# First two blocks of a fused attention and feed-forward kernel in halves of eight slots

## The chip, the cores and the metric

The kernel runs on one core of a Trainium2 chip. The metric is the device time of one execution in microseconds, the median of several runs. The engines are TensorE (PE, matmuls into PSUM), VectorE (DVE), ScalarE (ACT, functions by tables), GpSimd (POOL) and SyncE (SP, which issues the transfers).

## The reference

A linear attention with a complex decay, then two feed-forward layers on 3072 tokens of 384 features:

```python
scale = np.minimum(mag, 0.999) / (mag + 1e-06)      # mag = |a_re + i a_im|
for t in range(S):                                   # S = 768, B = 4, H = 8, D = 48
    S_re = ar * S_re - ai * S_im + k_t (x) v_t
    S_im = ar * S_im + ai * S_re_old
    y[:, :, t] = q_t . S_re
x = y as (3072, 384)
h = x @ w_in;  x = (h * cos(h)) @ w_out              # d_ff = 2048
h = x @ w2_in; y = (h * sigmoid(h)) @ w2_out
```

The weights come as 64-bit floats.

## The kernel before

**Attention in chunks.** Tokens go in 24 chunks of 128 (NC); chunk c belongs to batch c % 4. For a chunk, PE sums logarithms and angles over time with a triangular matrix (XL, XU: tiles pl, pu), DVE and ACT make the exponentials and the sine and cosine of the angles (FR, XE, XM, XS), DVE forms kt and qt (KQ), PE transposes them (TR: pt) and makes scores (SC: ps), DVE masks these into A, PE forms the output (YY: py) and the new state (PS: pS), and XF splits py into two 16-bit parts, xhi on ACT and xlo on DVE. ACT's exponentials and its sines use different tables, and LOGS and TRIG load them.

**Feed-forward in blocks and slots.** Three chunks make a block u of 384 tokens (8 blocks). Layer 1 of a block takes 16 slots, one for each piece f of 128 of the 2048 hidden features. In a slot, G1 makes h (nine matmuls: three pieces of the 384 features, each as hi x hi, lo x hi, hi x lo), GA takes the cosine on ACT, as a sine with a shift, GB multiplies (DVE) and rounds to ghi (ACT), GC forms the remainder glo (DVE), and two slots later G2 adds ghi and glo times w_out into three accumulators acc in PSUM (nine matmuls). h has two buffers, so h of slot s + 2 waits for glo of slot s. After f = 15, G2 copies the accumulators to o and stores them to x1d in DRAM; layer 2 reads them from there.

**Weights of layer 1.** RAW1 loads the 64-bit weights of a piece f (786 KB); DVE decodes them in three steps (lines 421, 423, 425) into wd, ACT rounds to 16 bits (line 456), DVE makes the remainder (line 466). A call `run` advances this stream by so many steps; four steps are one piece.

**Order.** PE and ACT run in the order in which the code issues. DVE, POOL and SP are ordered by a scheduler at build time, from slot 0 on. A table `plan` says what is called in which slot, half 0 ahead of G2 and half 1 behind it: chunk c starts at slot base(c), with XLU (XL, XU, FR) there, the tables, XE, XM and the next chunk's logarithms XA in half 1, the sines and KQ one slot on. TR(c - 1) and TR(c) stand relative to base: the transposes of k of chunk c at base(c + 1) - 2, those of q at base(c + 1) - 1. Before, base is 2, 6, 10, 14, 19 for chunks 4 to 8 (line 608). Tiles of the tag "a" in PSUM (pt, ps, py, pS, pl, pu, pn) share three buffers.

Of the kernel before, what the change touches and what calls it, by code (L numbers as in the profile page):

```python
# [9 lines left out]
F32 = mybir.dt.float32  # L10
# [44 lines left out]
GBUFS, WBUFS = 3, 3  # L55
SPARE = {(2, 1): 4, (2, 0): 5, (1, 2): 6, (2, 2): 7, (1, 3): 8, (1, 1): 9, (1, 6): 9, (1, 5): 10, (2, 5): 11, (2, 6): 12, (2, 3): 13, (2, 4): 14, (3, 0): 15}
LEADS = (2, 3, 4, 6, 7)
NA = 12
# [8 lines left out]
def fast_path(tc, q, k, v, a_re, a_im, w1_in, w1_out, w2_in, w2_out, out, bad_cnt):  # L67
    nc = tc.nc
    act, V, PE, G, SP = nc.scalar.activation, nc.vector, nc.tensor, nc.gpsimd, nc.sync
    with ExitStack() as ctx:  # L70
# [25 lines left out]
        x1d = dr.tile([NBLK, 128, KT, TB], F32, name="x1d")  # L96

# [149 lines left out]
        def XSP(c):  # L247
            d = st[c]
            if c < NFP:
                return  # L250
            ahi, thi = (xp.tile([128, DM], F32R, name=n, bufs=1) for n in ("ahi", "thi"))
            alo, tlo = (yp.tile([128, DM], F32R, name=n, tag=t) for n, t in (("alo", "ip"), ("tlo", "f")))
            act(out=ahi, in_=d["a1"], func=AF.Copy)
            act(out=thi, in_=d["an"], func=AF.Copy, scale=1.0 / TWO_PI)
            G.tensor_tensor(out=alo, in0=d["a1"], in1=ahi.bitcast(F32), op=ALU.subtract)
            V.scalar_tensor_tensor(out=tlo, in0=d["an"], scalar=1.0 / TWO_PI, in1=thi.bitcast(F32), op0=ALU.mult, op1=ALU.subtract)
            d["split"] = (ahi, alo, thi, tlo)
# [11 lines left out]
        def FR(c):  # L269
            d = st[c]  # L270
            pu = d["pu"]
            f = d["f"] = new(c, "f", yp)
            cs = d["cs"] = new(c, "cs", yp, cols=2 * DM).rearrange("p (h c d) -> p h c d", h=H, c=2)
            if CPU <= c < NFP:
                act(out=f, in_=pu, func=AF.Copy, bias=MAGIC)
            else:
                V.tensor_scalar(out=f, in0=pu, scalar1=MAGIC, scalar2=None, op0=ALU.add)
            V.scalar_tensor_tensor(out=f, in0=f, scalar=MAGIC, in1=pu, op0=ALU.subtract, op1=ALU.subtract)  # L278
            if c + B < NC:
                SP.dma_start(out=card[c % B:c % B + 1, :], in_=f[127:128, :])  # L280
            V.tensor_scalar(out=cs[:, :, 0].bitcast(I32), in0=hd(f).bitcast(I32), scalar1=0x7FFFFFFF, scalar2=None, op0=ALU.bitwise_and)
# [87 lines left out]
        def XF(c):  # L369
            u, cu = divmod(c, CPU)  # L370
            if cu == 0:
                xts[u] = tuple(xt.tile([128, KT, TB], F16, name=n) for n in ("xhi", "xlo"))
# [167 lines left out]
        def G2(layer, u, f, g):  # L540
            w = W[layer, f]
            if f == 0:
                acc[layer, u] = [px.tile([128, TB], F32, name=f"acc{m}") for m in range(KT)]
            for m, n in [(m, n) for m in range(KT) for n in range(2)] + [(m, 2) for m in range(KT)]:
# [5 lines left out]
                PE.matmul(out=acc[layer, u][m], lhsT=lhsT, rhs=rhs, start=(f == 0 and n == 0), stop=(f == NF - 1 and n == 2))  # L550
            if f == NF - 1:
                for m, ps in enumerate(acc.pop((layer, u))):
                    o = stage.tile([128, TB], F32, name="o", bufs=3)
                    sc = p2(SX1 - SG - SWT) if layer == 0 else p2(-SG2 - SWT)
                    if m == 1:
# [3 lines left out]
                    if layer == 0:  # L559
# [7 lines left out]
        def X1(u):  # L567
            hi, lo = (xt.tile([128, KT, TB], F16, name=n) for n in ("xhi", "xlo"))
# [39 lines left out]
        def base(c):  # L608
            return (16 * (c - CPU)) // 3 - LEADS[min(c - CPU, len(LEADS) - 1)]

# [24 lines left out]
        at(0, 1, XS, CPU)  # L635
        at(1, 0, KQ, CPU)
        for c in range(CPU, NC):
            b0 = base(c)
            if c > CPU:
                if c + 1 < NC:  # L640
                    at(b0 - 1, 1, XQ, c + 1)
                    at(b0 - 1, 1, XR, c + 1)
# [13 lines left out]
                at(b0 + YO, YH, YYS, c - 1)  # L656
                at(b0 + XFO, 1, XF, c - 1)
# [18 lines left out]
        for n in range(24):  # L676
            at(n, 0, run, 2)
            at(n, 1, run, 2)
# [23 lines left out]
        def slot(s):  # L702
            if 0 <= s < last:
                layer, r = divmod(s, 16 * NBLK)
                u, f = divmod(r, 16)
# [323 lines left out]
```

## Time and profile before

| | us |
|---|---|
| runs shown, median (lowest to highest) | 1006.39 (1005.92 to 1006.64) |
| the profiled execution | 1005.74 |
| its span, first to last instruction | 1004.0 |
| PE busy | 954.7 (95%) |
| VectorE busy | 624.2 (62%) |
| ScalarE busy | 606.9 (60%) |
| POOL busy | 114.9 (11%) |
| mean granted clock of PE | 0.986 |

The profile is taken by the hardware from one execution. The page cuts the span in 40 slices of 25.1 us. Its other views used here are the list of waits (who waited for whom, as semaphores tell), the timeline of an engine, windows (busy times in a stretch) and the chain of waits that ended last. [...] Slot 0 starts at 49.96 us, slot 2 at 68.46, slot 9 at 114.56 and slot 16 at 151.66.

### The profile page before, as it was taken

What the parts mean: (1) busy time and instruction counts of PE and PEld (TensorE: products, weight loads), DVE (VectorE), ACT (ScalarE), POOL (GpSimd) and SP (SyncE); (2) the same over time, 40 slices, a digit from 0 to 9 for tenths busy, and PEclk for the clock granted to TensorE, in tenths of its full rate; (3) what the DMA queues carried; (4) which work ended last, traced back from release to release, by engine and by line L of the source; (5) the groups of instructions that cost most, each with busy time, mean ns of one, the idle gap of its engine ahead of it and who ended that gap; (6) DMA issues with size and microseconds to landing.
All of it is one profiled execution on the core that took longest, in us unless ns stands there. A gap on an engine that the chain in (4) does not pass through costs nothing.

```text
span 1004.0 us, 19089 instructions
## 1 busy us (share of the span) xinstructions
PE 954.7 (95%) x7442; PEld 633.7 (63%) x7442; DVE 624.2 (62%) x1171; ACT 606.9 (60%) x1195; POOL 114.9 (11%) x136
## 2 busy tenths in 40 slices
PE   2959999999999999999999998999999999999997
PEld 1736677777777777777766655666666666666664
DVE  6899976666666666666667498734344434377541
ACT  7768887777777777787873455444444444444432
POOL 0112432222222222222200000000000000000000
PEclk9959999999999999999999999999999999999999
DMA  9892223123122222222114235324444454445410
GB/s 222 226 292 49 41 50 75 39 56 70 37 48 64 41 64 41 41 65 40 26 48 142 79 109 158 113 70 144 142 149 136 148 150 146 138 131 153 134 40 27
DMA packets 167987, 98.97 MB, mean 99 GB/s; under 512 B 130984, under 2 KB 152528, under 8 KB 167888
## 3 DMA queue, kind: packets, MB, share of 16 engines
q1 hardware_dynamic: 167888, 97.67, 35.8%
q8 instruction: 60, 0.98, 0.4%
q14 instruction: 39, 0.32, 0.1%
HBM read 88.11 MB, written 9.47 MB: 97 GB/s over the span
## 4 chain that ended last, share of the span: by engine, by line
PE 81%; DVE 8%; ACT 4%; DMA 3%; SPq 2%; issue 1%; ACTq 0%; DVEq 0%
PE h L511 33%; PE acc L550 32%; PE py L352 4%; PE pt L321 4%; PE ps L330 3%; PE pS L361 3%; SPq L166 2%; DMA raw<-in_moe_w_in_dram 1%; DVE wd L423 1%; DMA w<-in_moe_w_in_dram 1%; DVE wd L425 1%; DVE glo L533 1%; DMA raw<-in_moe_w_out_dram 1%; DVE wd L421 1%; DVE h L526 1%
## 5 line engine op out<-in xcount | busy, mean ns | idle before, releaser
L511 PE MATMUL h<-xhi,w 128*128 128x384 f16 x1536 | 376.6, 327 | 9.4 <-DVE glo L533 8.8
L511 PEld LDWEIGHTS <-w 128*128 128x128 f16 x2304 | 221.3, 98 | 152.7 <-issue 15.4
L511 PE MATMUL h<-xlo,w 128*128 128x384 f16 x768 | 251.4, 327 | 0.8 <-DVE xlo L378 0.8
L520 ACT ACTIVATE g<-h 128x384 f32<-128x384 f32 x128 | 62.8, 491 | 161.8 <-PE h L511 161.6
L550 PEld LDWEIGHTS <-w 128*128 128x128 f16 x1152 | 110.8, 98 | 69.0 <-issue 3.7
L550 PE MATMUL acc<-ghi,w 128*128 128x384 f16 x768 | 146.0, 326 | 0.0
L550 PE MATMUL acc<-w,ghi 128*128 128x384 f16 x768 | 145.7, 326 | 0.0
L535 DVE SCALAR_TENSOR_TENSOR glo<-g,ghi 128x384 f16<-128x384 f32 x128 | 70.9, 554 | 110.2 <-ACT ghi L528 109.8
L518 ACT ACTIVATE g<-h,hpi 128x384 f32<-128x384 f32 x128 | 74.3, 580 | 105.2 <-PE h L511 105.2
L526 DVE SCALAR_TENSOR_TENSOR h<-h,g 128x384 f32<-128x384 f32 x128 | 72.0, 563 | 61.8 <-ACT g L518 61.8
L550 PEld LDWEIGHTS <-ghi 128*128 128x128 f16 x768 | 75.2, 98 | 49.6
L533 DVE TENSOR_TENSOR glo<-h,ghi 128x384 f16<-128x384 f32 x128 | 70.4, 550 | 53.1 <-ACT ghi L528 52.0
L528 ACT ACTIVATE ghi<-g 128x384 f16<-128x384 f32 x128 | 66.8, 522 | 41.4 <-PE acc L550 37.3
L528 ACT ACTIVATE ghi<-h 128x384 f16<-128x384 f32 x128 | 62.2, 486 | 36.0 <-DVE h L526 32.0
L550 PE MATMUL acc<-glo,w 128*128 128x384 f16 x384 | 83.3, 326 | 0.0
L550 PE MATMUL acc<-w,glo 128*128 128x384 f16 x384 | 83.3, 326 | 0.0
L550 PEld LDWEIGHTS <-glo 128*128 128x128 f16 x384 | 37.6, 98 | 24.8
L189 POOL TENSOR_TENSOR a<-a,a 128x384 f32<-128x384 f32 x21 | 31.0, 1477 | 155.4 <-ACT a L185 155.4
L352 PE MATMUL py<-A,v 128*32 128x128 f32 x704 | 43.2, 279 | 4.3 <-DVE A L331 3.9
L330 PE MATMUL ps<-qY,kY 96*128 96x128 f32 x352 | 43.4, 275 | 0.2 <-DVE f L278 0.2
L330 PEld LDWEIGHTS ps<-qY,kY 96*128 96x128 f32 x352 | 42.3, 192 | 1.9 <-DVE f L278 0.6
L352 PE MATMUL py<-qY,S 96*32 96x128 f32 x640 | 40.8, 274 | 0.0
(183 smaller groups left out, 1264.7 us busy)
## 6 DMA issues: line engine op xcount, KB each, us to landing
rawc<-in_moe_w_in_dram SPq DMA_DIRECT2D x32, 384.0 KB
rawc<-in_moe_w_out_dram SPq DMA_DIRECT2D x32, 384.0 KB
w<-in_moe_w_in_dram SPq DMA_DIRECT2D x16, 384.0 KB
w<-in_moe_w_out_dram SPq DMA_DIRECT2D x16, 384.0 KB
raw<-in_moe_w_in_dram SPq DMA_DIRECT2D x16, 384.0 KB
raw<-in_moe_w_out_dram SPq DMA_DIRECT2D x16, 384.0 KB
x1d<-o SPq DMA_DIRECT2D x24, 192.0 KB
x1f<-x1d SPq DMA_DIRECT2D x24, 192.0 KB
```

Source lines behind the costliest of these rows:

```text
L189: EN().tensor_tensor(out=a1, in0=a1, in1=a2, op=ALU.add)
L321: PE.transpose(pt[:, h, :], src[:, 4 * g + h].rearrange("p c d -> p (c d)"), idt)
L330: PE.matmul(out=ps[:, h, :], lhsT=d["kY"][:, 4 * g + h, :], rhs=d["qY"][:, 4 * g + h, :], start=True, stop=True)
L352: PE.matmul(out=py[32 * q:32 * q + 32, kk, :], lhsT=lhsT, rhs=rhs, start=q not in others[:i], stop=q not in others[i + 1:])
L511: PE.matmul(out=h, lhsT=w[:, wp, kk * 128:(kk + 1) * 128], rhs=x[xpart][:, kk, :], start=(n == 0), stop=(n == 3 * KT - 1))
L518: act(out=g, in_=h, func=AF.Sin, scale=p2(-SX - SWT), bias=hpi)
L520: act(out=g, in_=h, func=AF.Silu, scale=p2(-SX1 - SWT))
L526: V.scalar_tensor_tensor(out=h, in0=h, scalar=p2(SG - SX - SWT), in1=g, op0=ALU.mult, op1=ALU.mult)
L528: act(out=hi, in_=g, func=AF.Copy, scale=1.0 if layer == 0 else p2(SG2))
L533: V.tensor_tensor(out=lo, in0=g, in1=hi, op=ALU.subtract)
L535: V.scalar_tensor_tensor(out=lo, in0=g, scalar=p2(SG2), in1=hi, op0=ALU.mult, op1=ALU.subtract)
L550: PE.matmul(out=acc[layer, u][m], lhsT=lhsT, rhs=rhs, start=(f == 0 and n == 0), stop=(f == NF - 1 and n == 2))
```

## The change

The slots of layer 1 come in a new order for the first two blocks: pieces 0 to 7 of block 0, pieces 0 to 7 of block 1, pieces 8 to 15 of block 0, pieces 8 to 15 of block 1 (table ORD). After the first half of a block, the accumulators are stored to a DRAM tile `part`; after the second half they are added to what is loaded from there, by three DVE operations in place of two copies on ACT and one on DVE. So block 1 needs its attention, chunks 3 to 5, by slot 8 instead of slot 16: base is 1, 4, 7, 13, 19 for chunks 4 to 8, and YY, PS and XF of chunk 5 move into slot 7. XS and KQ of chunk 3 move ahead in slots 0 and 1. Decode steps are four a slot for five slots and then three, for up to 40 slots, instead of four for 24. The wd tile has two buffers instead of three, f two instead of one, and xhi and xlo three instead of two.

```diff
--- before.py
+++ after.py
@@ -52,9 +52,12 @@
 TK, TKH, TQ, TQH = -2, 0, -1, 0
 CKS, SPS = 2, 2
 DW, SW, SH, RW = 7, 3, 0, 10
-GBUFS, WBUFS = 3, 3
+GBUFS, WBUFS = 3, 2
 SPARE = {(2, 1): 4, (2, 0): 5, (1, 2): 6, (2, 2): 7, (1, 3): 8, (1, 1): 9, (1, 6): 9, (1, 5): 10, (2, 5): 11, (2, 6): 12, (2, 3): 13, (2, 4): 14, (3, 0): 15}
+EARLY = {3: -2, 4: 1, 5: 4, 6: 7, 7: 13, 8: 19}
 LEADS = (2, 3, 4, 6, 7)
+ORD = ([(0, u, 8 * half + f) for half in range(2) for u in range(2) for f in range(8)]
+       + [(0, u, f) for u in range(2, NBLK) for f in range(NF)] + [(1, u, f) for u in range(NBLK) for f in range(NF)])
 NA = 12
 NX, NW, NR, N1 = 3 * NA, 3 * NA + NC, 3 * NA + NC + 2 * NF, 3 * NA + NC + 4 * NF
 NCHK = N1 + NC
@@ -94,6 +97,7 @@
 
         card = dr.tile([B, DM], F32, name="card")
         x1d = dr.tile([NBLK, 128, KT, TB], F32, name="x1d")
+        part = dr.tile([2, 128, KT, TB], F32, name="part")
 
         idt = const.tile([128, 128], F32, name="idt")
         U = const.tile([128, 128], F32, name="U")
@@ -249,7 +253,7 @@
             if c < NFP:
                 return
             ahi, thi = (xp.tile([128, DM], F32R, name=n, bufs=1) for n in ("ahi", "thi"))
-            alo, tlo = (yp.tile([128, DM], F32R, name=n, tag=t) for n, t in (("alo", "ip"), ("tlo", "f")))
+            alo, tlo = (yp.tile([128, DM], F32R, name=n, tag=t, bufs=b) for n, t, b in (("alo", "ip", 1), ("tlo", "f", 2)))
             act(out=ahi, in_=d["a1"], func=AF.Copy)
             act(out=thi, in_=d["an"], func=AF.Copy, scale=1.0 / TWO_PI)
             G.tensor_tensor(out=alo, in0=d["a1"], in1=ahi.bitcast(F32), op=ALU.subtract)
@@ -269,7 +273,7 @@
         def FR(c):
             d = st[c]
             pu = d["pu"]
-            f = d["f"] = new(c, "f", yp)
+            f = d["f"] = new(c, "f", yp, bufs=2)
             cs = d["cs"] = new(c, "cs", yp, cols=2 * DM).rearrange("p (h c d) -> p h c d", h=H, c=2)
             if CPU <= c < NFP:
                 act(out=f, in_=pu, func=AF.Copy, bias=MAGIC)
@@ -369,7 +373,7 @@
         def XF(c):
             u, cu = divmod(c, CPU)
             if cu == 0:
-                xts[u] = tuple(xt.tile([128, KT, TB], F16, name=n) for n in ("xhi", "xlo"))
+                xts[u] = tuple(xt.tile([128, KT, TB], F16, name=n, bufs=3) for n in ("xhi", "xlo"))
             hi, lo = (t[:, :, cu * C:(cu + 1) * C] for t in xts[u])
             py = st[c]["py"]
             m = sqs[c] = sqp.tile([128, DM], BF16, name="m", tag="sq", bufs=3)
@@ -539,7 +543,10 @@
 
         def G2(layer, u, f, g):
             w = W[layer, f]
-            if f == 0:
+            split = layer == 0 and u < 2
+            first = f == 0 or split and f == NF // 2
+            final = f == NF - 1 or split and f == NF // 2 - 1
+            if first:
                 acc[layer, u] = [px.tile([128, TB], F32, name=f"acc{m}") for m in range(KT)]
             for m, n in [(m, n) for m in range(KT) for n in range(2)] + [(m, 2) for m in range(KT)]:
                 a, b = PASS[n]
@@ -547,16 +554,21 @@
                     lhsT, rhs = w[:, a, DM + m * 128:DM + (m + 1) * 128], g[b]
                 else:
                     lhsT, rhs = g[b][:, m * 128:(m + 1) * 128], w[:, a, DM:]
-                PE.matmul(out=acc[layer, u][m], lhsT=lhsT, rhs=rhs, start=(f == 0 and n == 0), stop=(f == NF - 1 and n == 2))
-            if f == NF - 1:
+                PE.matmul(out=acc[layer, u][m], lhsT=lhsT, rhs=rhs, start=(first and n == 0), stop=(final and n == 2))
+            if final:
                 for m, ps in enumerate(acc.pop((layer, u))):
                     o = stage.tile([128, TB], F32, name="o", bufs=3)
                     sc = p2(SX1 - SG - SWT) if layer == 0 else p2(-SG2 - SWT)
-                    if m == 1:
+                    if split and f == NF - 1:
+                        SP.dma_start(out=o, in_=part[u, :, m, :])
+                        V.scalar_tensor_tensor(out=o, in0=ps, scalar=sc, in1=o, op0=ALU.mult, op1=ALU.add)
+                    elif m == 1:
                         V.tensor_scalar(out=o, in0=ps, scalar1=sc, scalar2=None, op0=ALU.mult)
                     else:
                         act(out=o, in_=ps, func=AF.Copy, scale=sc)
-                    if layer == 0:
+                    if split and f < NF - 1:
+                        SP.dma_start(out=part[u, :, m, :], in_=o)
+                    elif layer == 0:
                         SP.dma_start(out=x1d[u, :, m, :], in_=o)
                     else:
                         ci, b = divmod(CPU * u + m, B)
@@ -565,7 +577,7 @@
         x1s = {}
 
         def X1(u):
-            hi, lo = (xt.tile([128, KT, TB], F16, name=n) for n in ("xhi", "xlo"))
+            hi, lo = (xt.tile([128, KT, TB], F16, name=n, bufs=3) for n in ("xhi", "xlo"))
             for kk in range(KT):
                 t = stage.tile([128, TB], F32, name="x1f", tag="o", bufs=3)
                 SP.dma_start(out=t, in_=x1d[u, :, kk, :])
@@ -606,6 +618,8 @@
             V.tensor_copy(out=bad_cnt, in_=cnt)
 
         def base(c):
+            if c in EARLY:
+                return EARLY[c]
             return (16 * (c - CPU)) // 3 - LEADS[min(c - CPU, len(LEADS) - 1)]
 
         plan = {}
@@ -632,14 +646,14 @@
 
         at(0, 0, XU, CPU)
         at(0, 0, FR, CPU)
-        at(0, 1, XS, CPU)
-        at(1, 0, KQ, CPU)
+        at(0, 0, XS, CPU)
+        at(0, 0, KQ, CPU)
         for c in range(CPU, NC):
             b0 = base(c)
             if c > CPU:
                 if c + 1 < NC:
-                    at(b0 - 1, 1, XQ, c + 1)
-                    at(b0 - 1, 1, XR, c + 1)
+                    at(max(b0 - 1, 0), int(b0 > 0), XQ, c + 1)
+                    at(max(b0 - 1, 0), int(b0 > 0), XR, c + 1)
                 at(b0, 0, XLU, c)
                 at(b0, 1, LOGS)
                 at(b0, 1, XEM, c)
@@ -653,8 +667,8 @@
                 if c + 1 < NC:
                     at(b0 + 1, 0, XT, c + 1)
                     at(b0 + 1, 0, XC, c + 1)
-                at(b0 + YO, YH, YYS, c - 1)
-                at(b0 + XFO, 1, XF, c - 1)
+                at(b0 + (0 if c == 6 else YO), 1 if c == 6 else YH, YYS, c - 1)
+                at(b0 + (0 if c == 6 else XFO), 1, XF, c - 1)
                 at(b0 + XFO + 2, 1, XN, c - 1)
             if c + 1 < NC:
                 at(b0 + SPS, 0, XSP, c + 1)
@@ -673,9 +687,9 @@
         for f in range(NF):
             if f >= 7:
                 at(max(f - RW, 0), 0, RAW1, f)
-        for n in range(24):
+        for n in range(40):
             at(n, 0, run, 2)
-            at(n, 1, run, 2)
+            at(n, 1, run, 2 if n < 5 else 1)
         at(W2S[0] - 2, 0, RAW2, 0)
         at(W2S[0] - 2, 0, RAW2, 1)
         for n in range(2 * NF):
@@ -701,8 +715,7 @@
 
         def slot(s):
             if 0 <= s < last:
-                layer, r = divmod(s, 16 * NBLK)
-                u, f = divmod(r, 16)
+                layer, u, f = ORD[s]
                 assert layer or f in done
                 h = G1(layer, u, f)
             mid = None
```

What the change moves, at three places on which terms rest. Line numbers are each kernel's own; in the change those of the functions above are four higher (h is L515, pt L325, ps L334, py L356, pS L365) and from G2 on seven.

PE, the slots 1 and 2: behind h of slot 1, before (pn is a norm of three matmuls of width 1):

```order
L511 MATMUL h<-xlo,w 128x384
L388 LDWEIGHTS m
L388 MATMUL pn<-ones,m 128x1
L388 LDWEIGHTS m
L388 MATMUL pn<-ones,m 128x1
```

and in the change:

```order
L515 MATMUL h<-xlo,w 128x384
L325 MATMUL pt<-idt,kt 96x128 x8
L325 MATMUL pt<-idt,qt 96x128 x8
L245 MATMUL pl<-a_522,U 128x384
L267 MATMUL pu<-im,U_108 128x384
L334 MATMUL ps<-qY,kY 128x128 x8
L392 LDWEIGHTS m
```

Chunk 3's transposes, chunk 4's sums and chunk 3's scores moved ahead of h of slot 2.

PE, behind the outputs of chunk 3 (py, pS), before:

```order
L511 MATMUL h<-xlo,w 128x384
L352 MATMUL py<-A,v 32x128 x16
L361 MATMUL pS<-v,kt 96x48 x8
L550 LDWEIGHTS w
L550 MATMUL acc_752<-ghi,w 128x384
```

and in the change, where kt is that of chunk 4:

```order
L515 MATMUL h<-xlo,w 128x384
L356 MATMUL py<-A,v 32x128 x16
L365 MATMUL pS<-v,kt 96x48 x8
L325 MATMUL pt<-idt,kt 96x128 x8
L557 LDWEIGHTS w
L557 MATMUL acc_832<-ghi,w 128x384
```

The transposes of chunk 4's k moved up by a slot, directly behind pS of chunk 3.

DVE, from glo of slot 9 to glo of slot 10, before (f, cs and k are chunk 6's, A is chunk 5's):

```order
L533 TENSOR_TENSOR glo<-h,ghi 128x384
L425 SCALAR_TENSOR_TENSOR wd<-w,wd 128x768
L526 SCALAR_TENSOR_TENSOR h<-h,g 128x384
L278 SCALAR_TENSOR_TENSOR f<-f,pu 128x384
L466 SCALAR_TENSOR_TENSOR w<-wd,w 128x768
L281 TENSOR_SCALAR cs<-f 128x8x48
L331 TENSOR_TENSOR A<-ps,U 128x512 x2
L297 TENSOR_TENSOR k<-k,pl 128x384
L204 SCALAR_TENSOR_TENSOR a_1277<-a_1277 128x384
L205 SCALAR_TENSOR_TENSOR a_1276<-a_1277,a_1276 128x384
L533 TENSOR_TENSOR glo<-h,ghi 128x384
```

and in the change:

```order
L537 TENSOR_TENSOR glo<-h,ghi 128x384
L427 SCALAR_TENSOR_TENSOR wd<-w,wd 128x768
L530 SCALAR_TENSOR_TENSOR h<-h,g 128x384
L425 TENSOR_SCALAR wd<-w 128x768
L393 COPY chk<-pn 128x1
L429 SCALAR_TENSOR_TENSOR wd<-w,wd 128x768
L427 SCALAR_TENSOR_TENSOR wd<-w,wd 128x768
L429 SCALAR_TENSOR_TENSOR wd<-w,wd 128x768
L470 SCALAR_TENSOR_TENSOR w<-wd,w 128x768
L537 TENSOR_TENSOR glo<-h,ghi 128x384
```

Where attention stood with two decode operations (L425, L466) there are now six (L427 and L429 twice, L425, L470), and no attention.

## Rows read from the trace of the kernel before

**Rows 1.** Page, part 2: busy tenths and granted clock in 40 slices.

```profile
PE   2959999999999999999999998999999999999997
...
PEclk9959999999999999999999999999999999999999
```

**Rows 2.** Windows: length, busy time (x instructions) by engine, PEclk, DMA share, GB/s.

```profile
62.90:114.50 51.60, 42.48 (x347) 30.10 (x346) 51.60 (x82) 40.53 (x71) 14.28 (x9) 0.89 0.41 97
114.50:151.60 37.10, 36.33 (x358) 26.72 (x357) 29.98 (x50) 32.12 (x60) 12.37 (x10) 1.00 0.20 40
```

**Rows 3.** Waits of PE, 62 to 114.5 us: total, times, longest.

```profile
PE h L511 <- DVE glo L533: 5.4, 1, 5.4
PE py L352 <- DVE A L331: 1.5, 1, 1.5
PE pt L321 <- ACT kY L322: 0.7, 1, 0.7
PE pt L321 <- DVE chk L389: 0.6, 1, 0.6
PE py L352 <- DVE k L297: 0.4, 1, 0.4
PE pn L388 <- DVE A L331: 0.3, 1, 0.3
PE ps L330 <- DVE f L278: 0.2, 1, 0.2
```

**Rows 4.** Timeline of PE: start, us, instruction, [idle before <-releaser].

```profile
58.48 1.65 PE L263 MATMUL pu<-w,U 128*128 128x384 f32 x2 [5.93 <-ACT w L229]
...
68.46 0.80 PE L511 MATMUL h<-xhi,w 128*128 128x384 f16 x2 [5.39 <-DVE glo L533]
...
71.29 1.92 PE L321 MATMUL pt<-idt,kt 128*96 128x128 f32 x8
...
73.00 1.68 PE L321 MATMUL pt<-idt,qt 128*96 128x128 f32 x8
...
81.88 1.45 PE L352 MATMUL py<-A,v 128*32 128x128 f32 x32 [0.38 <-DVE k L297]
```

**Rows 5.** Windows of PE: length, busy (x), PEclk, DMA share, GB/s.

```profile
54.00:56.00 2.00, 0.00 (x0) 0.50 1.07 365
...
74.00:76.00 2.00, 2.00 (x11) 0.93 0.03 12
```

**Rows 6.** Chain of waits, 143 to 157 us: start, us, what.

```profile
143.44 1.78 PE ps L330 x16
...
145.23 1.47 PE h L511 x9
...
146.69 2.18 PE py L352 x64
...
148.87 1.49 PE pS L361 x16
...
156.21 0.87 PE pt L321 x8
```

**Rows 7.** Timeline of ACT, chunk 4, 76 to 86 us.

```profile
76.00 0.49 ACT L275 ACTIVATE f<-pu 128x384 f32<-128x384 f32 x1 [0.70 <-PE pu L263]
...
84.95 0.61 ACT L304 ACTIVATE cs<-cs,hpi 128x384 f32<-128x384 f32 x1
```

**Rows 8.** Timeline of DVE, 116 to 120 us.

```profile
117.46 0.54 DVE L421 TENSOR_SCALAR wd<-w 128x768 int32<-128x768 int32 x1
117.92 0.55 DVE L526 SCALAR_TENSOR_TENSOR h<-h,g 128x384 f32<-128x384 f32 x1
118.39 0.94 DVE L425 SCALAR_TENSOR_TENSOR wd<-w,wd 128x768 int32<-128x768 int32 x1
119.26 0.94 DVE L423 SCALAR_TENSOR_TENSOR wd<-w,wd 128x768 int32<-128x768 int32 x1
```

**Rows 9.** Timeline of PE, 540 to 565 us.

```profile
546.84 0.43 PE L352 MATMUL py<-A,v 128*32 128x128 f32 x8 [2.42 <-DVE A L331]
```

## The prediction

> **What bounds the kernel now.** I read the page first: TensorE (PE) is busy in nine tenths or more of nearly every slice; only the first three slices have gaps and a lowered clock [rows 1]. A reordering of two blocks can therefore win back only what PE loses early, so I next asked for engine totals from 62.9 to 114.5 us, the stretch of slots 2 to 8. There VectorE (DVE) is busy for all 51.60 us, and PE for 42.48; from 114.5 to 151.6 PE misses only 37.10 - 36.33 = 0.8 us [rows 2]. The list of waits says what PE waited for in the first stretch: once 5.4 us for a glo, then six small waits, 1.5 + 0.7 + 0.6 + 0.4 + 0.3 + 0.2 = 3.7 us, all but one for DVE [rows 3]. The timeline shows two large holes: 5.93 us before pu of chunk 3, which ACT's arctangent releases, and 5.39 us before h of slot 2 [rows 4]. [...]
>
> PE's instructions are the same number and kinds after the change, and the order up to h of slot 1 is the same on every engine. So the hole of 5.93 us and the slow clock from 54 us stay. What can change is: 5.4 + 3.7 + 0.8 = 9.9 us of later waits, and what new waits the denser attention brings.
>
> **Durations.** On PE at full clock: nine matmuls of h or of acc 1.47, ps 1.78, py with a state 2.18, without 1.4, pS 1.49, one half of a chunk's transposes 0.87 [rows 4, 6]. On DVE an operation of 768 elements takes 0.87 from its start to the next one's, one of 384 elements and the first decode step 0.47 [rows 8].
>
> **Chunk 3 drawn forward: -1.3 us.** Its transposes now stand before h of slot 2. They wait for kt of chunk 3, which DVE can make when the sines are there: after f (62.7), the second decode pair and the mask operation DVE reaches kt at 66.0 and ends it at 66.9. PE then starts at 67.0 with the transposes where it used to stand until 68.46 for glo. The hole from 63.07 shrinks from 5.39 to about 4.0. Transposes, pl and pu of chunk 4 took PE from 71.29 to 76.00 before, 4.7 us, the clock rising on the way [rows 4, 5, 7]; they start closer to the last work now, so I give them 5.6, up to 72.6.
>
> **Chunk 4: +4.1 us.** In each chunk the transposes of k need kt, kt needs the sines, and these stand in ACT's queue behind a fixed list: f, a weight copy, table load, two exponentials, five logarithms and exponentials of the next chunk, table load, ghi, g. In the trace of before this list runs without a gap from 76.00 to 84.95 + 0.61 = 85.56, which is 9.6 us [rows 7]; with kt 10.5. Before, PE had two slots for that time: acc, ps, h, py, pS, acc, h = 4 x 1.47 + 1.78 + 1.4 + 1.49 = 10.6. After, TR(4) stands one slot after XLU(4), and PE has only ps, h, py, pS: 1.78 + 0.2 + 1.47 + 1.4 + 1.49 = 6.4. PE waits 10.5 - 6.4 = 4.1, from about 79 to 83 us; acc of slot 0 and h of slot 3, which have all they need, are queued behind the transposes.
>
> **Chunk 5: +2.1, and its end: +0.9.** One slot again: acc, ps, h, py, pS = 2 x 1.47 + 1.78 + 2.18 + 1.49 = 8.4 against 10.5, so 2.1, part of it at py (for A), the rest at the transposes. In slot 7, ps and py of chunk 5 stand directly behind each other; py waits about 0.9 for DVE's two masked copies, which stand behind k of chunk 6.
>
> **Gone: -3.5.** Of the six small waits 3.5 belong to positions that are filled or counted anew; one of 0.2 (ps for f) recurs.
>
> Slots 1 to 8: -1.3 + 4.1 + 2.1 + 0.9 - 3.5 = **+2.3**.
>
> **Slots 9 to 12: +0.7.** No attention stands here for PE but two transposes, while DVE still decodes three steps a slot. From kt of chunk 6, which can start 1.5 after h of slot 8 (g, then two sines on ACT), to glo of slot 10 DVE has 12.6 us of queued work: nine operations at 0.87, ten at 0.47 (each first decode step is one of them) and a small copy, 9 x 0.87 + 10 x 0.47 + 0.07. That is 14.1 after h of slot 8. PE reaches h of slot 12, which needs that glo's buffer, after seven groups of nine, one transpose half and a norm, 11.2. So up to 2.9 of waiting; the lower end is 0, if DVE reaches this stretch with decode steps already done. I take the middle, 1.5, because the same engine mix from 114.5 on cost 0.8 [rows 2]. Less those 0.8: +0.7.
>
> **Clock: +1.5.** [...] Before, PE worked from 68.46 to about 74.2, 5.7 us, before the clock rose [rows 4, 5]; at half rate that costs 2.9. I take half of it; the ends are 0 and 2.9.
>
> [...]
>
> **Partial sums: +0.3.** Twelve transfers of 192 KB (six out, six in); the DMA engines are 0.20 busy from 114.5 us [rows 2], and the loads have eight slots of lead. The accumulators are emptied at slots 9, 17, 25 and 33 instead of 17 and 33. The next acc stands behind an h of 1.47 us, and three copies are spread over ACT and DVE, so nothing shows there; at 25 and 33 all three are on DVE, 3 x 0.47, which has spare time by then. Ends: 0, and 6 x 0.47 = 2.8 if PE waited for each; I take 0.3. Fewer wd buffers cost nothing: DVE runs the decode steps of one tile in order, and the buffer is free when its last reader, on DVE too, has passed. The second f buffer and the third x buffer take away waits that the list of PE's waits does not show: 0.
>
> **Sum:** 2.3 + 0.7 + 1.5 + 0.3 = +4.8 on the profiled 1005.74 is 1010.5. The median of the runs shown, 1006.39, lies 0.65 above that execution, so I forecast **1011.2 us**.
>
> **Rivals.**
> *DVE's relief decides (faster).* DVE is full from 62.9 to 114.5 [rows 2], and the pace falls from four decode steps a slot to three from slot 5. If kt of chunk 4 is done by 80 us, TR(4) and TR(5) wait at most 1 each: -1.3 - 3.5 - 0.8 + 2.0 = -3.6, 1002.8. Against it: ACT's list of 9.6 us had no gap in it, so less DVE work cannot shorten it [rows 7]. 0.18.
> *Old waits against new (no change).* The sum of slots 1 to 8 holds, slots 9 to 12 run without a wait, the clock stays up: 2.3 - 0.8 = +1.5, 1007.9. 0.18.
> *The emptying of accumulators is on the path.* DVE's three sums stand at slot 25 in front of chunk 9's cs and A; if PE waits for each, 2.8 in place of 0.3, and about 0.5 at the two extra emptyings: +7.8 with the rest, 1014.2. For it: A is what py waits for in the rows of waits [rows 3]. 0.10.
> *The clock falls at each new wait.* Two more restarts, before TR(5) and at py of chunk 5, at the 1.5 of the first: +3.0, 1014.2. Against it: the wait of 2.42 us [rows 1, 9]. [...] 0.12.
> The forecast keeps 0.42.
>
> **How the numbers follow.** Faster than 1006.4 by over 0.2% (2.0 us, about what a measurement of this kernel can tell) comes from the first rival, 0.18; within 0.2% from the second, 0.18; slower from the other three, 0.64. The forecast's own bounds: clock 0 to 2.9, slots 9 to 12 -0.8 to +2.1, sums 0 to 2.8, so +1.5 to +10.1. The range takes in the faster rival's 1002.8 and both slow ones, and ends at 1015.0; beyond lie the forecast's worst bounds together.
>
> **What would show it.** Right: a wait of 3 to 5 us of PE before the first pt of chunk 4, released by DVE's kt; one of 1 to 2 before chunk 5's; a granted clock of 0.50 somewhere from 80 to 90 us; the hole before pu of chunk 3 unchanged at 5.9; DVE no longer at 51.60 of 51.60. Wrong: PE's waits from 62 us to slot 16 sum to less than 10 us, or kt of chunk 4 ends before pS of chunk 3. Waits of acc at slots 10 and 18, or of py at 26, would speak for the third rival.

## The result, and the profile after

The changed kernel takes 1016.55 us (median of 4 runs, 1015.8 to 1018.75), the kernel before, run beside it, 1006.15 (1005.28 to 1006.64): a ratio of 1.0111, 95% interval 1.0098 to 1.0123. It is slower, as forecast, but by twice as much: the forecast was 4.8 us over the kernel before and its range ended at 1015.0. The profiled execution took 1017.3 us with a span of 1015.6, against 1004.0 before. These two executions differ by 11.6 us, 1.2 more than the medians; what follows accounts for the 11.6.

Page of the change, part 2, the lines that answer to [rows 1]:

```profile
PE   2857889999999999999999998999999999999997
...
PEclk9968999999999999999999999999999999999999
```

The gaps of TensorE (PE) now reach into the sixth slice (127 to 152 us), and its clock is low in the fourth too (6 and 8 tenths of full speed in the third and fourth, before 5 and 9). Windows of the change, same stretches and columns as [rows 2]:

```profile
62.90:114.50 51.60, 40.16 (x328) 29.60 (x329) 46.37 (x70) 39.32 (x71) 10.11 (x10) 0.86 0.41 97
114.50:151.60 37.10, 32.18 (x256) 22.38 (x255) 31.29 (x51) 25.87 (x46) 5.95 (x6) 0.95 0.22 49
```

VectorE (DVE), full in the first stretch before, now idles 51.60 - 46.37 = 5.2 us of it, while PE idles 2.3 us more than before. In the second stretch PE idles 4.9 where it idled 0.8. The forecast expected VectorE to come off its full 51.60; that VectorE would itself have to wait while PE waits for it is what it had not seen.

Where the time went can be read from one window per kernel. From pu of chunk 3 to pu of chunk 23 both kernels do nearly the same work (the four stored and reloaded half sums apart); windows before:

```profile
58.48:515.74 457.26, 447.04 (x3990) 319.27 (x3991) 317.15 (x540) 345.79 (x648) 104.35 (x109) 0.98 0.26 59
515.74:1004.00 488.26, 476.67 (x3190) 291.45 (x3189) 263.54 (x565) 217.04 (x469) 1.19 (x1) 1.00 0.39 119
```

and of the change:

```profile
57.96:525.73 467.77, 450.63 (x3991) 321.37 (x3991) 323.04 (x546) 346.19 (x648) 96.36 (x109) 0.98 0.28 63
525.73:1015.60 489.87, 478.36 (x3190) 291.97 (x3189) 264.32 (x565) 216.63 (x469) 1.19 (x1) 0.99 0.40 118
```

The stretch is 10.5 us longer. PE's idle time in it, length less busy time, went from 10.2 to 17.1 (+6.9), and PE's busy time grew by 3.6. Of that, 3.0 is matmuls at the lower clock, as worked out below; the other 0.6 is not traced further. Behind the stretch come another 1.6, and in front of it the change is 0.5 ahead: 10.5 + 1.6 - 0.5 = 11.6, the difference of the spans.

The waits of PE in the change, from its timeline (columns as in [rows 4]; the waits of [rows 3] answer to them):

```profile
57.96 1.65 PE L267 MATMUL pu<-w,U 128*128 128x384 f32 x2 [5.94 <-ACT w L233]
66.53 1.92 PE L325 MATMUL pt<-idt,kt 128*96 128x128 f32 x8 [4.04 <-DVE kt L316]
72.83 1.16 PE L334 MATMUL ps<-qY,kY 96*128 96x128 f32 x8 [0.38 <-DVE f L282]
82.46 1.94 PE L325 MATMUL pt<-idt,kt 128*96 128x128 f32 x8 [4.41 <-DVE kt L316]
96.68 2.10 PE L334 MATMUL ps<-qY,kY 96*128 96x128 f32 x16 [1.13 <-DVE f L282]
101.99 0.31 PE L356 MATMUL py<-A,v 128*32 128x128 f32 x3 [0.53 <-DVE A L335]
105.71 0.61 PE L325 MATMUL pt<-idt,kt 128*96 128x128 f32 x4 [0.68 <-DVE kt L316]
107.01 0.64 PE L325 MATMUL pt<-idt,kt 128*96 128x128 f32 x4 [0.68 <-ACT kY L326]
118.06 2.10 PE L334 MATMUL ps<-qY,kY 96*128 96x128 f32 x16 [0.88 <-DVE f L282]
121.31 0.43 PE L356 MATMUL py<-A,v 128*32 128x128 f32 x8 [1.16 <-ACT a L202]
131.75 0.48 PE L515 MATMUL h<-xhi,w 128*128 128x384 f16 x2 [0.85 <-DVE glo L537]
140.88 0.48 PE L515 MATMUL h<-xhi,w 128*128 128x384 f16 x2 [1.97 <-DVE glo L537]
```

Behind the first they sum to 16.7 us; before, the waits from pu of chunk 3 to slot 16 were 9.9. The line of 121.31 names ScalarE's L202 as releaser, but that one, 0.51 us long, had started at 120.18; what ended as py started is VectorE's first mask operation for A, behind k of chunk 6 as forecast (timeline of VectorE):

```profile
120.07 0.54 DVE L301 TENSOR_TENSOR k<-k,pl 128x384 f32<-128x384 f32 x1
120.53 1.28 DVE L335 TENSOR_TENSOR A<-ps,U 128x512 f32<-128x512 f32 x2
```

The clock fell twice, within the wait of 4.41 (from 80.5 us on, with PE idle) and just behind that of 1.97 (windows of the change):

```profile
80.00:82.00 2.00, 0.00 (x0) 0.00 (x0) 2.00 (x5) 1.56 (x4) 0.00 (x0) 0.62 0.11 22
82.00:84.00 2.00, 1.54 (x8) 1.48 (x9) 1.74 (x3) 0.42 (x1) 0.00 (x0) 0.50 0.19 37
84.00:86.00 2.00, 2.00 (x8) 1.04 (x7) 0.21 (x1) 1.74 (x4) 0.00 (x0) 0.50 0.83 160
86.00:88.00 2.00, 2.00 (x12) 1.08 (x11) 1.84 (x5) 1.04 (x3) 0.00 (x0) 0.67 0.00 0
...
140.00:142.00 2.00, 1.12 (x7) 0.68 (x7) 1.97 (x5) 0.80 (x2) 0.00 (x0) 0.98 0.00 0
142.00:144.00 2.00, 2.00 (x10) 1.57 (x8) 2.00 (x4) 0.77 (x2) 0.00 (x0) 0.50 0.00 0
144.00:146.00 2.00, 2.00 (x10) 1.20 (x9) 0.56 (x2) 1.74 (x4) 0.00 (x0) 0.66 0.00 0
```

As an estimate, a fall costs busy time times (1 - clock), summed over half-microsecond windows: 2.4 us for the first (78 to 100 us), 1.7 for the second (138 to 150). Counted alike, the low clock at the start cost 4.1 us in the change and 5.2 before, so the clock's part of the loss is 2.4 + 1.7 - 1.1 = 3.0.

Why VectorE idles shows at chunk 4's transposes. VectorE in the change (start, length):

```profile
82.33 0.94 DVE L316 TENSOR_TENSOR qt<-cs,q 128x768 f32<-128x768 f32 x1
83.20 0.54 DVE L239 SCALAR_TENSOR_TENSOR im<-car,im 1x384 f32<-1x384 f32 x1
85.79 0.96 DVE L470 SCALAR_TENSOR_TENSOR w<-wd,w 128x768 f16<-128x768 f32 x1 [2.06 <-ACT w L460]
```

and ScalarE (ACT) at the same time:

```profile
83.58 0.59 ACT L326 ACTIVATE kY<-pt 96x512 f32<-96x512 f32 x1 [2.03 <-PE pt L325]
84.44 0.59 ACT L326 ACTIVATE kY<-pt 96x512 f32<-96x512 f32 x1 [0.26 <-PE pt L325]
84.93 0.83 ACT L460 ACTIVATE w<-wd 128x768 f16<-128x768 f32 x1
```

PE waits for VectorE's kt; ScalarE waits for PE's transposes, to copy them; behind the copies stands the rounding of a weight piece (L460); and VectorE, having given kt, has that piece's remainder (L470) next, so it waits for ScalarE. A wait of 4.41 us on PE comes back to the engine that caused it as 2.06 us of idle time. L460 did not start before the copies of 83.58 and 84.44, though the last decode step of its piece (L429, 0.94 us from 78.73) had ended at 79.7: in these rows ScalarE kept the order of the code.

### The profile page after: what moved, and what is told of

Same layout as the page of the kernel before. It is cut to its first block, busy times and chain, and to the rows that moved or that the text cites. A ratio compares the mean times of both kernels' runs of the same rounds, so it can differ in the third digit from the quotient of the medians.

```text
span 1015.6 us, 19117 instructions
## 1 busy us (share of the span) xinstructions
PE 960.0 (95%) x7442; PEld 636.4 (63%) x7442; DVE 630.9 (62%) x1177; ACT 607.0 (60%) x1195; POOL 107.0 (11%) x136
## 4 chain that ended last, share of the span: by engine, by line
PE 80%; DVE 8%; ACT 5%; DMA 4%; issue 2%; SPq 1%; POOL 0%; DVEq 0%; ACTq 0%; POOLq 0%
PE h L515 33%; PE acc L557 32%; PE pt L325 4%; PE py L356 4%; PE ps L334 3%; PE pS L365 2%; DMA raw<-in_moe_w_in_dram 1%; DVE wd L427 1%; DVE wd L429 1%; DVE glo L537 1%; DMA w<-in_moe_w_out_dram 1%; ACT L179 1%; DMA rawa<-in_a_re_dram 1%; ACT p L291 1%; DMA w<-in_a_im_dram 1%
## 5 line engine op out<-in xcount | busy, mean ns | idle before, releaser
L515 PE MATMUL h<-xhi,w 128*128 128x384 f16 x1536 | 376.1, 327 | 6.2 <-DVE glo L537 6.0
L515 PEld LDWEIGHTS <-w 128*128 128x128 f16 x2304 | 221.2, 98 | 149.4 <-issue 11.3
L515 PE MATMUL h<-xlo,w 128*128 128x384 f16 x768 | 251.2, 327 | 0.8 <-DVE xlo L382 0.8
L557 PE MATMUL acc<-ghi,w 128*128 128x384 f16 x768 | 148.4, 330 | 0.0
L356 PE MATMUL py<-A,v 128*32 128x128 f32 x704 | 42.8, 279 | 3.9 <-DVE A L335 2.7
L334 PE MATMUL ps<-qY,kY 96*128 96x128 f32 x352 | 43.7, 276 | 2.4 <-DVE f L282 2.4
L334 PEld LDWEIGHTS ps<-qY,kY 96*128 96x128 f32 x352 | 42.3, 192 | 4.4 <-DVE f L282 3.0
L356 PE MATMUL py<-qY,S 96*32 96x128 f32 x640 | 40.9, 274 | 0.0
L193 POOL TENSOR_TENSOR a<-a,a 128x384 f32<-128x384 f32 x21 | 22.6, 1075 | 170.7 <-ACT a L189 170.7
```

The lines of the kernel that those rows point to most:

```text
L193: EN().tensor_tensor(out=a1, in0=a1, in1=a2, op=ALU.add)
L334: PE.matmul(out=ps[:, h, :], lhsT=d["kY"][:, 4 * g + h, :], rhs=d["qY"][:, 4 * g + h, :], start=True, stop=True)
L356: PE.matmul(out=py[32 * q:32 * q + 32, kk, :], lhsT=lhsT, rhs=rhs, start=q not in others[:i], stop=q not in others[i + 1:])
L515: PE.matmul(out=h, lhsT=w[:, wp, kk * 128:(kk + 1) * 128], rhs=x[xpart][:, kk, :], start=(n == 0), stop=(n == 3 * KT - 1))
```

## The experiments

Ratios are to the kernel before, run beside each kernel on the same chip. "To chunk 23" is the stretch from pu of chunk 3 to pu of chunk 23 of the profiled execution, where the kernel before takes 457.3 us (10.2 idle on PE, 447.0 busy) and the change 467.8 (17.1 and 450.6). Each kernel has one profiled execution, so its columns can stand above or below what the median says.

| kernel | median us | ratio (95%) | to chunk 23 | PE idle | PE busy |
|---|---|---|---|---|---|
| e3 early attention, no halves | 1016.98 | 1.0099 (1.0083 to 1.0115) | 466.7 | 16.6 | 450.1 |
| e4 halves' sums alone | 1008.99 | 1.0019 (1.0011 to 1.0028) | 458.0 | 10.8 | 447.2 |
| e1 transposes later | 1013.44 | 1.0064 (1.0046 to 1.0082) | 463.8 | 15.6 | 448.2 |
| e2 slower decode | 1017.61 | 1.0104 (1.0086 to 1.0121) | 467.0 | 16.0 | 451.0 |
| e5 both of these | 1011.26 | 1.0054 (1.0038 to 1.0071) | 461.9 | 15.0 | 446.9 |
| e10 rounding first | 1014.3 | 1.0079 (1.0062 to 1.0096) | 466.6 | 15.9 | 450.7 |
| e14 cut at 10 | 1011.5 | 1.0047 (1.0032 to 1.0063) | 462.0 | 13.8 | 448.2 |
| e6 cut at 12 | 1007.27 | 1.0011 (1.0002 to 1.0021) | 458.7 | 11.6 | 447.1 |
| e12 cut at 13 | 1007.53 | 1.0007 (0.9998 to 1.0016) | 458.1 | 10.8 | 447.2 |
| e8 buffers alone | 1003.83 | 0.9976 (0.9965 to 0.9986) | 455.4 | 8.5 | 446.9 |
| e13 second f alone | 1007.0 | 1.0007 (0.9998 to 1.0016) | 457.1 | 10.6 | 446.6 |
| e11 buffers, slower decode | 1008.8 | 1.0019 (1.0010 to 1.0028) | 457.9 | 10.8 | 447.1 |

**Which part costs: e3 and e4.** e3 is the change in the old slot order, without the stored half sums and at the old pace of decode:

```diff
-ORD = ([(0, u, 8 * half + f) for half in range(2) for u in range(2) for f in range(8)]
...
+ORD = [(layer, u, f) for layer in range(2) for u in range(NBLK) for f in range(NF)]
...
-            split = layer == 0 and u < 2
+            split = False
```

> The attention of chunks 3 to 5 as early as in the change, but the slots in the old order, no partial sums, and the old decode pace of four steps a slot for 24 slots. Theory A (the early attention itself makes the waits): the wait before chunk 4's transposes is 4 to 5 us as in the change, the clock falls there, and PE is 5 to 7 us behind the kernel before at slot 9; 1009 to 1014 in all. Theory B (the halves and what goes with them cost): within 1.5 us of the kernel before, 1005 to 1007.5.

e4 is the kernel before with the accumulators of blocks 0 and 1 stored after piece 7 and added after piece 15 (the `split` lines of the change), the order of slots, the attention and the buffers as before.

> The kernel before with the accumulators of blocks 0 and 1 stored to DRAM after slot 7 of each block and added back after slot 15; order of slots, attention and decode as before. Theory A: the twelve transfers and the sums on DVE are hidden, 0 to 1 us slower than before, 1006 to 1007.2. Theory B (DVE's sums or the emptying of accumulators stand on the path): PE waits at acc or py behind slots 9, 17, 25 and 33, 2.8 us slower or more, 1009 or more.

The early attention alone makes nearly the whole loss: +9.4 us to chunk 23 against +10.5 of the change, with nearly the same waits (4.04, 4.61, 1.13, 0.65 and 0.68, 0.85, 1.71). Its time, 1016.98, lies even above theory A's 1014. The half sums cost 0.7 to chunk 23. e4's median, 1008.99, lies outside theory A's range and at the lower edge of B's, but its trace shows no wait at acc up to chunk 23 and those of py for A are the 1.5 us of before, so B's mechanism is not in it. e4's profile ends 3.3 us later than that of before. Behind chunk 23, where e4 changes nothing, the lower clock costs 3.2 us in two falls, one around the last py of the attention (546.85), one behind the wait at the first slot of layer 2 (616.85). Whether the other executions lose their time there too isn't shown. Windows of e4 (its first fall) and then of before, the same matmul py with the same cause (a wait of 2.86 and of 2.42 us for A) inside:

```profile
545.00:550.00 5.00, 3.15 (x60) 2.89 (x62) 4.59 (x10) 0.00 (x0) 0.00 (x0) 0.66 0.42 136
```

```profile
545.00:550.00 5.00, 3.17 (x68) 2.71 (x69) 4.58 (x10) 0.53 (x2) 0.00 (x0) 1.00 0.41 137
```

**Where it sits: e1, e2, e5.** e1 issues the k transposes of chunks 4 and 5 one slot later:

```diff
-            at(base(c + 1) + (TK if c > CPU else 0), TKH, TR, c, "k")
+            at(base(c + 1) + (-1 if c in (4, 5) else TK if c > CPU else 0), TKH, TR, c, "k")
```

> The change with the k transposes of chunks 4 and 5 one slot later (beside those of q). Theory A (PE's queue holds acc and h behind transposes that wait for ACT's list of 9.6 us, and the clock falls in that wait): acc of slot 0 and h of slot 3 (2.9 us) fill the wait of 4.41 us before the transposes of chunk 4, 1 to 1.5 us of it stay; the granted clock stays at 1.00 from 72 us to slot 9, which gives back 2.1 us; 4 to 6 us faster than the change, 1010.5 to 1012.5. Theory B (DVE's work, decode beside denser attention, sets the pace of slots 1 to 8): the wait moves to f, A or glo, less than 1 us is won, 1015.5 or more.

Its median is 3.1 us below that of the change; by the ratios, each to the kernel before run beside it, it is 1.0111 less 1.0064, 4.7 us; to chunk 23 it is 4.0. The median lies outside both ranges, and the size is nearer theory A's. The wait of 4.41 and the clock fall behind it are gone (PE busy to chunk 23 falls by 2.4), but idle time falls by 1.6 only: other waits come up in its place, 1.57 for a glo at 80.60 and 1.21 for f at 92.32 among them. e2 takes one decode step a slot out from slot 5 on:

```diff
-            at(n, 0, run, 2)
+            at(n, 0, run, 2 if n < 5 else 1)
```

> The change with two decode steps a slot instead of three from slot 5 on. Theory A (from slot 9 to 12 PE waits because decode steps stand between two glo in DVE's queue, and the clock falls there again): the waits for glo of 0.85 and 1.97 us fall under 1 us together, the clock stays at 1.00 around slot 12, 3 to 4.5 us faster than the change, 1012 to 1013.5; the waits for f of chunks 5 and 6 (1.13, 0.88) shrink too. Theory B (those waits come from the chunk's own chain): less than 1 us, 1015.5 or more.

No gain, as theory B had it. The waits of 0.88 and 1.16 at chunk 5's end go, but one of 2.18 for glo at 131.98 comes, with a clock fall behind it, and from 158 to 164 us PE idles 1.5 us while VectorE is full, decode steps among its work. e5 has both edits:

> The change with chunk 4's and 5's k transposes one slot later and with two decode steps a slot from slot 5 on instead of three, both edits of earlier runs in one kernel. Theory A (VectorE's backlog sets slots 5 to 12): the 3.1 us of the later transposes stay and the two waits of chunk 6 (0.9 and 1.2), which the slower decode took away, go too: 1011.0 to 1012.5. Rival B (the slower decode only moves the wait to slot 10 and beyond, as it did alone): 1013.0 to 1014.5.

The median lies in theory A's range; by the ratios, 1.0064 less 1.0054, the second edit gives 1.0 us of the 2 it should (1.9 to chunk 23), and the two intervals overlap, so this gain isn't shown by the times. From 70 us to chunk 23 its clock stays at 1.00 (busy 446.9, as before): with the clock out of the way, 15.0 - 10.2 = 4.8 us of waits are the price that stays.

**Is it VectorE's idle time: e10.** The change with the decode steps of a half slot planned ahead of everything else in it (the loop with `run` moved in front of the loop over chunks), so that L460 stands before the copies of the transposes.

> The change, with the decode steps of a half slot written ahead of everything else planned there, so that ScalarE's rounding of a weight piece (L460) stands before the copies of the transposes of that half, not behind them. Theory A: VectorE is what everything waits for up to slot 12, and it idles 5.2 us of the 64 us from 58 to 122, 4 of them in front of remainders (L470) whose rounding stands behind those copies. Then its idle time before L470 falls from 5.5 to under 1.5 and the time by 3 to 5 us: 1011.5 to 1013.5. Rival B: the idle time of VectorE only follows from the ring VectorE's kt, TensorE's transposes, ScalarE's copies, which the edit leaves as it is: ScalarE then waits for the decode instead, the wait before chunk 4's transposes stays above 3.5, and the time stays at 1015.5 to 1017.5.

Between the theories: some 2 us below the change by medians, 3 by ratios. The profiled execution took 1016.75, the slowest of the four and 2.45 above their median, so where those 2 to 3 us were won, its trace can't show. In it, VectorE's idle time before L470 fell from 5.5 to 1.5 us as A said. Its idle time as a whole did not: windows from pu of chunk 3 to glo of slot 12, of the change and then of e10:

```profile
57.96:147.23 89.27, 72.49 (x565) 50.48 (x566) 79.16 (x124) 63.12 (x114) 15.39 (x16) 0.87 0.39 95
```

```profile
58.00:146.72 88.72, 73.14 (x569) 50.55 (x570) 78.57 (x123) 62.81 (x114) 16.09 (x16) 0.89 0.39 96
```

10.1 us both times (89.27 - 79.16, 88.72 - 78.57). What VectorE no longer waits for, ScalarE does: its waits for the last decode step (wd, L429) grew from 3.7 to 7.1 us, and the hole before chunk 3's transposes from 4.04 to 5.19; the wait before chunk 4's fell to 3.34, where B wanted 3.5 or more. In this execution, then, the idle time goes with the ring of the three engines, as in rival B, and not with one place in an order. That a ring is behind all of it is argued from this and from the rows above, not shown by an edit that opens it. In the kernel before, the window up to glo of slot 12 had almost none:

```profile
58.48:136.81 78.33, 68.43 (x555) 47.61 (x556) 76.43 (x123) 61.11 (x109) 23.31 (x15) 0.90 0.40 97
```

1.9 us of 78.33. The change puts 79.16 - 76.43 = 2.7 us more of VectorE's work ahead of that glo and 8.2 us more of its idle time; together they are the 10.9 us by which that glo comes later.

**How much earlier: e14, e6, e12.** The halves are cut at slot 10, 12 and 13 instead of 8, so that block 1's attention is needed that much later; e14:

```diff
-EARLY = {3: -2, 4: 1, 5: 4, 6: 7, 7: 13, 8: 19}
+EARLY = {3: -2, 4: 2, 5: 5, 6: 9, 7: 14, 8: 19}
+HS = 10
...
```

> The change with its halves cut at slot 10 instead of 8: ten slots of block 0, ten of block 1, then six and six, and the attention drawn forward by less, chunks 4, 5 and 6 at slots 2, 5 and 9 instead of 1, 4 and 7 (2, 6 and 10 in the kernel before). Theory A: the loss is that of VectorE's and ScalarE's work pushed before slot 8, so it shrinks with the distance: between the cut at 12 (1007.3) and at 8 (1016.5), 1009.5 to 1013. Rival B: the loss comes from the three slots between chunks 4 and 5, too few for the ring from table to transposes to copies; these are three here too, so most of the loss stays: 1013.5 to 1016.5.

Theory A: 1011.5, though chunks 4 and 5 stand three slots apart as in the change. Its largest waits are 6.16 at slot 2's glo, 3.30 before chunk 4's transposes and 1.21 for f. e6 (cut at 12, one buffer for f, slower decode):

> The halves cut at slot 12 instead of 8: twelve slots of block 0, twelve of block 1, then four and four; attention as before except the end of chunk 5, one slot earlier; three decode steps a slot up to slot 7 (four at 8 to 10), then one; two wd buffers, one f buffer, three for x. Theory A: it is the attention drawn forward that costs, and the halves themselves let 10 to 13 decode steps (8 to 11 us of VectorE) leave the first twelve slots, so that the small waits up to slot 12 shrink from 9 us of before by 3 or more, against 0.7 to 2 for the partial sums: 1003 to 1006. Rival B: the waits of slots 1 to 4 are not VectorE's backlog and stay, block 1 is just late at slot 12 and waits 1 to 3 us, and the partial sums cost their 2: 1008 to 1011.

1007.27, between the two. Slot 8's glo is 4.3 us earlier than before, counted from pu of chunk 3 (54.2 against 58.5), but slot 10's is where it was (71.13 against 71.11). e12 (cut at 13, attention as before, the two f and two wd buffers of the change, slower decode):

> The halves cut at slot 13, attention exactly as in the kernel before, three decode steps a slot up to slot 7, four at 8 to 11, then one; two buffers for f, two for the decoded weights, three for x. Theory A: with the attention left where it was, the halves cost only their partial sums (0.7 to 2), the buffers give 1.8 and the slower decode 1 to 3: 1001 to 1005, below the kernel before. Rival B: as with the cut at 12, what the slower decode gives up to slot 8 is lost again between slots 8 and 13, where block 1 must be there: 1005.5 to 1008.

No difference that can be measured, as in rival B. So the loss grows with the number of slots by which the attention comes forward: 0.07% with none and 0.11% with the end of chunk 5 one slot earlier, which noise does not tell apart, then 0.47% at cut 10 and 1.1% at cut 8. Pace of decode and buffers differ among these too: e6 and e12 decode more slowly than the change, and e6 has one buffer for f.

**The buffers: e8, e13, e11.** e8 has the kernel before with two wd buffers instead of three and two for f instead of one:

```diff
-GBUFS, WBUFS = 3, 3
+GBUFS, WBUFS = 3, 2
...
-            f = d["f"] = new(c, "f", yp)
+            f = d["f"] = new(c, "f", yp, bufs=2)
```

> The kernel before with only the buffers of the change (two for f instead of one, two for the decoded weights instead of three). Theory A: no order of work on TensorE and ScalarE moves, and no wait of the trace of before is for one of these buffers: 1005 to 1007.5. Rival B: with two wd buffers the decode of a piece waits for the remainder of the piece two before it, which adds waits of VectorE before L425 and costs 2 us or more: 1008 to 1012.

Faster than the forecast of either theory, and than the kernel before: 0.9976 (0.9965 to 0.9986). e13 has f's buffer alone:

> The kernel before with a second buffer for f alone; three for the decoded weights as before. Theory A: of the 1.8 us that both buffers gave, the second buffer for f gives all: 1003 to 1004.5. Rival B: it was the third buffer of the decoded weights that cost (the order of VectorE's decode steps follows from it), and f's buffer gives nothing: 1005 to 1006.5.

Rival B: nothing. So the gain is tied to the second edit, the third wd buffer taken away; that edit alone wasn't run, but the program that it alone gives has the same order on every engine as e8, while e13's has that of the kernel before. Between e8 and the kernel before, only VectorE's order differs, and it tells how the edit can help. Around f of chunk 4 the scheduler has three pieces in their second and third steps at once in the kernel before, two in e8:

```
before: L421 x2, L533 glo, L421, L423 x3, L526, L425 x3, L278 f, L466, L331 A, L281 cs
e8:     L421, L533 glo, L421, L423 x2, L425, L526, L425, L278 f, L281 cs, L466, L331 A
```

With fewer pieces in flight f and A stand behind less decode: f of chunk 4 starts 17.9 us behind pu of chunk 3 in e8 and 19.3 in the kernel before. The waits of py for A between 62 and 150 us fall from 1.5 to 0.2 us, and PE's idle time to chunk 23 from 10.2 to 8.5. e11 adds to e8 three decode steps a slot instead of four in slots 0 to 7:

> The kernel before with the two buffers changed (two for f, two for the decoded weights) and three decode steps a slot instead of four in slots 0 to 7, no halves and no earlier attention. Theory A: VectorE is full up to slot 8 and TensorE waits for it, so taking 8 steps (6 to 7 us of VectorE) out of slots 0 to 7 brings slot 8 2 to 4 us earlier, and half of that stays to the end, since VectorE has room from slot 9 on: 1000 to 1003. Rival B: the decoded weights then come too late for their slots between 8 and 15 and what was gained is waited for there: 1003.5 to 1006.

It misses both theories on the slow side. Slot 8's glo is 3.7 us earlier than in the kernel before (54.86 against 58.51 from pu of chunk 3), and slot 12's 0.8 later (79.15 against 78.33): what was gained up to slot 8 is lost again between slots 8 and 12, and more. e12, with these buffers and this pace and the halves besides, is not slower than e11 (1.0007 against 1.0019).

## Why the prediction was wrong in size

Its direction and its first mechanism hold: PE does wait before the transposes of chunks 4 and 5 for work that stands in ScalarE's and VectorE's lists, and the signs that it named for being right all came. The steps that failed are sizes in its sum: the waits for f (0.2, measured 2.4), the middle taken for slots 9 to 12 (1.5, measured 2.8), the half taken for the clock (1.5, measured 3.0), and the work behind chunk 23, for which it had no term (1.6). They make 6.6 of the 6.8 us between the forecast's 4.8 and the 11.6 of the profiled executions. Step by step:

- **What bounds the kernel.** Right that only the first slots can move. The hole before pu of chunk 3 stayed at 5.94.
- **Chunk 3, hole of about 4.0.** Measured 4.04. **Chunk 4, wait of 4.1 at 79 to 83 us.** Measured 4.41, ending at 82.46, released by kt. **Chunk 5, 2.1 in parts, and 0.9 at its end.** Measured 0.53 + 0.68 + 0.68 = 1.9, and 1.16. Counting ScalarE's list against PE's work (for the last, VectorE's masks) gave these four within some 0.3 us each. In chunk 4's count the parts of PE's work sum to 6.3, not 6.4, which changes nothing.
- **"One of 0.2 (ps for f) recurs": failed.** The scores waited for f three times, 0.38 + 1.13 + 0.88 = 2.4. VectorE's f stands behind decode steps, which the replay of ScalarE's list left out (timeline of VectorE in the change):

```profile
94.75 0.56 DVE L530 SCALAR_TENSOR_TENSOR h<-h,g 128x384 f32<-128x384 f32 x1
95.21 0.95 DVE L429 SCALAR_TENSOR_TENSOR wd<-w,wd 128x768 int32<-128x768 int32 x1
96.08 0.54 DVE L282 SCALAR_TENSOR_TENSOR f<-f,pu 128x384 f32<-128x384 f32 x1
```

- **"I take the middle, 1.5" in slots 9 to 12: failed.** The computed wait of 2.9 came in full: 0.85 + 1.97 = 2.82. The reason for halving it, that VectorE might reach the stretch with steps already done, did not apply: VectorE stood idle just before the kt from which the count starts, and from there worked almost without a gap to the end of glo of slot 10, 128.07 to 140.82, which is 12.75 us against the 12.6 counted (timeline of VectorE in the change):

```profile
128.07 0.96 DVE L316 TENSOR_TENSOR kt<-cs,k 128x768 f32<-128x768 f32 x1 [0.35 <-ACT cs L308]
...
140.27 0.55 DVE L537 TENSOR_TENSOR glo<-h,ghi 128x384 f16<-128x384 f32 x1
```

- **"I take half" of the clock: failed.** No run shows the half. In its place, the first fall cost 2.4 of the 2.9 that were its upper end, and there was a second of 1.7 after a wait of 1.97 us. Less the 1.1 that the start lost less than before, that is +3.0, twice the 1.5 of the sum. This and slots 9 to 12 (2.8 less the 0.8 of before, +2.0 of at most 2.1) both came in at their upper ends; the forecast's range left out that its bounds could be reached together, and here the second fall came right behind the wait at slot 12.
- **Partial sums, +0.3.** Up to chunk 23 they cost 0.7 (e4). No acc waits in the change. At the first slot of layer 2 the change lost 1.7 to a clock fall (0.50 from 627 to 630 us) behind a wait of 2.68 us for glo at 625.61, where before a wait of 2.10 had left the clock at 1.00; the forecast had no term for that. e10 waited 2.74 us at the same place and its clock stayed at 1.00, so the fall may belong to the execution and not to the change.
- **"Fewer wd buffers cost nothing ... 0": failed in the other direction.** In the kernel before they gave 1.8 us to chunk 23 (e8). If they give as much beside the early attention, which no run shows, that attention costs more than the net result: 1.0099 / 0.9976, an estimate of 1.2% or 12 us.

The sum again with what was measured: waits from 9.9 to 16.7 make +6.8 where the forecast had +3.0; clock +3.0 instead of +1.5; 0.7 of the stretch to chunk 23 is in neither; behind chunk 23 +1.6 and the start -0.5.

Of the rivals, *DVE's relief* is out: VectorE did come off its 51.60 of 51.60, but by waiting, and kt of chunk 4 ended at 82.4, not by 80. *Old waits against new* is out: the new waits and the clock both cost more than the sum, not less. The *accumulators* are out: in the change no wait of PE for them up to chunk 23. *The clock falls at each new wait* came nearest in time (1014.2), but not by its rule: of the eleven waits above behind the first, one found the clock low already and two lowered it, and the second fall came at slot 12, not before TR(5) or at py of chunk 5.

**What stays open.** Whether a ring makes all of VectorE's 10.1 us of idle time, which member of it sets e5's remaining 4.8 us of waits, and why VectorE's later decode in e11 costs more than it gave; none was tried further.

## What to carry to other kernels

When work of several engines is drawn forward, count every engine's list up to the new waits, not only the longest: here ScalarE's list gave the large waits to 0.3 us, and what was missing stood in VectorE's list (the waits for f and for glo, 3.5 us above the forecast) and in the clock (1.5, and 1.6 behind chunk 23). If an engine is full before a change and idle in places after it while the others wait for it, look for a ring of waits: there, moving one member can just move the wait (e10's trace). Fewer buffers can be faster where a scheduler uses a further buffer to start more of a side job at once: the best kernel of this study, 1003.83 us (ratio 0.9976, 0.9965 to 0.9986), is the one before with two wd and two f buffers, and none of the change's reordering.

## What the runs showed of the hardware

In these traces the clock did not follow the length of one wait. It fell to 0.50 just after a wait of 1.97 us (140.88 in the change) and to 0.66 over 5 us around one of 2.86 (546.85 in e4), and stayed at 1.00 around one of 2.42 at the same instruction in the kernel before [rows 9]. In e2 and e5 the same instruction, h of slot 10, waited 2.18 us; the clock fell to about 0.50 in e2 and stayed at 1.00 in e5. The waits, and the two microseconds behind them, e2 first:

```profile
131.98 0.76 PE L515 MATMUL h<-xhi,w 128*128 128x384 f16 x2 [2.18 <-DVE glo L537]
132.00:134.00 2.00, 2.00 (x7) 0.99 (x7) 2.00 (x4) 1.89 (x5) 0.00 (x0) 0.51 0.75 207
...
127.22 0.48 PE L515 MATMUL h<-xhi,w 128*128 128x384 f16 x2 [2.18 <-DVE glo L537]
127.00:129.00 2.00, 1.78 (x11) 1.07 (x11) 2.00 (x5) 2.00 (x5) 0.00 (x0) 1.00 0.64 165
```

In e3 the clock fell to 0.50 (107 to 110 us) right behind two waits of 0.65 and 0.68 us (106.26) and not behind one of 1.71 (141.30); the change had two waits of 0.68 us at the same place without a fall (1.00 from 100 to 140 us).

Behind pu of chunk 23 PE has the same 3190 matmuls in all these kernels (the end of layer 1, and layer 2). Falls there cost some 1.5 to 1.7 us each by the estimate above (1.5 and 1.7 in e4, 1.7 in the change), and there were none (before, e6), one (the change) or two (e4) in an execution. The stretch took 488.26 us before and from 487.95 (e6, no fall) to 491.99 (e4, two falls) in the others; e10 took 490.40 without a fall, so the clock is not all of it. Each kernel has one trace, so whether a fall belongs to a kernel or to an execution is open. A difference of 2 us between two profiled executions can be just that.
